# Attention stage of a three-block kernel: rounding, theta's high part and the sink columns move to GpSimd, the back-turned product stays in its own bank, and theta starts five steps later

## The chip, the cores and the metric

The kernel runs on one core of a Trainium2 chip. The metric is device time in microseconds (us) from the first to the last instruction of the program with what lies around it, and less is better. A kernel's time is the median of its runs.

## The reference, cut to what matters

```python
scores = q @ k.T / 8                    # 2 batches, 8 heads, 768 positions, 64 dims
scores = where(is_sink | in_window, scores, -1e9)        # 4 sink columns, window 128
a = softmax(scores);  x = a @ v         # x: 2 x 768 x 512
theta = x @ w_theta                     # 512 x 512
y = w_tok_r @ (x * cos(theta)) + w_tok_i @ (x * sin(theta))
u = x + y;  u = u + relu(u @ w_ch)
u = u + real(fft2(u));  out = u + relu(layernorm(u) @ w_ch1) @ w_ch2
```

Everything is fp32, and the inputs of each product except attention's are cut in a high and a low part (fp32r), so that a product is three matmuls: high by high, high by low, low by high.

## The kernel before, in words

The work has one order written out by hand, and a scheduler inside the language then settles the order on each engine from its own times. Attention (`attn_banded`) runs over 12 blocks of 128 positions (n, six for each batch; i is the block's number in its batch), four steps s to a block, and a loop over s issues, in each step, pieces of different blocks:

- `score_mms` at even steps: four heads' scores against the window (and sink) columns, in four PSUM banks (`ps_sc`). `scores` follows: VectorE adds the mask and finds the minimum (L515), ScalarE takes the exponential (L519). Once a block, for i of 2 or more, the sink columns of all heads are copied to `psk` (L524).
- `turn` one step later: TensorE transposes the probabilities of two heads into one of two banks (`ps_tp`, a ring), ScalarE or VectorE copies them out (L552). In a block's last turn the sink columns are transposed too, into the next bank of the same ring (L555), and copied to `pst` (L558).
- `av` six steps after the block's first step: the products with v into the bank `ps_acc` ("oa" in the rows). `av_turn` one step later transposes the product back, into a bank of `ps_tp`, and `normalize` (L608 to L610, VectorE) makes x from it.
- `theta_gen`, spread over four steps (and a rest that is issued when the next one starts): x is transposed into a bank of `ps_tp`, ScalarE makes the high part `hi` (L801) and the copy `xT` (L803), GpSimd (for the first nine tiles) the low part (L211), TensorE does twelve matmuls into the bank `th`, ScalarE copies them out scaled (L817), VectorE rounds to whole turns in two instructions (L818, L819) and GpSimd subtracts (L820).
- Until the first theta starts, each step has two dummy matmuls (L651) on zeros into the bank `th`; nothing reads them.
- Weights come as 64-bit words in `raw` tiles; `pump` converts one (`conv`: L279 on ScalarE, L287, L288, L291 on VectorE) and fetches the next on SyncE's queue (L255). The four tiles of w_theta are pumped at the steps of `THS` and cut in two one step later (ScalarE and GpSimd). From step `P0B` to `P0E`, every third step pumps a tile of w_tok. `conv` has a second form for `low_act`, used in later stages of the kernel before: ScalarE makes the low bits (L282), and VectorE needs two instructions (L283, L291) in place of three.

The step at which theta of tile u starts is `first(u) = 4u + AL + 2 + max(T1, T0 - u)`, with AL 3 and T1 4. With T0 of 7 that is 12, 15, 18, 21, then every fourth step. After attention come the token mixing (`y_gen`), the channel product, the transform and the MLP, all of them streams of matmuls.

Of the kernel before, what the change touches and what calls it, by code (L numbers as in the profile page):

```python
# [15 lines left out]
ALU = mybir.AluOpType  # L16
# [5 lines left out]
BLK = 128 + SINK  # L22
PW = 256 + SINK
BIG = 8.0e9
MAGIC = 12582912.0
# [4 lines left out]
GROUPS = [0, 3, 1, 2]  # L30
NSLOT = 67
NSLOT2 = 8
T0 = 7
DEPTH = 3
NRAW = 3
NJIT = 12
# [3 lines left out]
C1E = 12  # L40
TLC = 1
WN = 7
P0B = 15
P0N = 3
P0E = 40
F0 = 0
F1 = 2
ETH = 9
# [3 lines left out]
T1 = 4  # L52
TD = 1
AH = 5
THS = (5, 7, 9, 11)
P1E = 11
P2F = 1
TL = 1
# [132 lines left out]
class _Body:  # L191
# [315 lines left out]
    def scores(self, n, hp):  # L507
        nc = self.nc
        i, c = self.seq[n][1], n % 3
        nb, sm, p = self.tn[n]  # L510
        wd = PW if i else 128
        mask = self.masks[min(i, 2) if c else (0, 1, 3)[min(i, 2)]]
        for u, sc in enumerate(self.scs.pop((n, hp))):
            h = 2 * hp + u
            nc.vector.tensor_tensor_reduce(  # L515
                out=sc[:, 0:wd], in0=sc[:, 0:wd], in1=mask, op0=ALU.add, op1=ALU.min,
                scale=-0.125, scalar=3.0e38, accum_out=nb[:, h:h + 1],
            )
            self.last_exp = nc.scalar.activation(  # L519
                p[:, h, 0:wd], sc[:, 0:wd], AF.Exp, bias=nb[:, h:h + 1], scale=-1.0, accum_out=sm[:, h:h + 1]  # L520
            ).ins
        if hp == 3 and i >= 2:
            psk = self.psk.next()
            self.rnd("a", psk, p[:, :, 128:BLK])  # L524
            self.pt[n, 5] = psk
        if hp == 3:
            q = self.q.pop(n)
            if n:
                self.give(q)

    def turn(self, n, hp):
        nc = self.nc
        b, i = self.seq[n]
        c = n % 3
        p = self.tn[n][2]
        tp = self.ps_tp.next().rearrange("p (a m) -> p a m", a=4)
        pt = self.take(4, 128)
        parts = []
        for u in range(2):
            x, y = p[:, 2 * hp + u, 0:128], p[:, 2 * hp + u, BLK:PW]  # L540
            if i:
                prev, cur = (x, y) if c else (y, x)
                parts.append((u, prev, n - 1))
                parts.append((u, cur, n))
            else:
                parts.append((u, x, n))
        k = len(parts)
        for a, (u, pp, _) in enumerate(parts):
            self.tr(tp[:, a, :], pp, self.ident)
            yield  # L550
        tail = 4 * n + hp >= 4 * len(self.seq) - 5
        self.ev[n, hp] = self.rnd("v" if tail else EPT[hp], pt[:, 0:k], tp[:, 0:k])  # L552
        self.pt[n, hp] = pt, [(u, m) for u, _, m in parts]
        if hp == 3 and i >= 2:
            tp = self.ps_tp.next()  # L555
            self.tr(tp[:, 0:128], self.pt.pop((n, 5)).rearrange("p h c -> p (h c)"), self.ident)
            pst = self.pst.next()
            self.ev[n, 4] = self.rnd("v" if tail else "a", pst, tp[:, 0:128])  # L558
            self.pt[n, 4] = pst
# [35 lines left out]
        self.rnd("a", self.oT, acc)  # L595

    def av_turn(self, n):
        tp = self.ps_tp.next().rearrange("p (a m) -> p a m", a=4)
        for a in range(4):
            self.tr(tp[:, a], self.oT[:, a], self.ident)  # L600
        self.give(self.oT)
        self.normalize(*self.seq[n], tp.rearrange("p a m -> p (a m)"), self.tn.pop(n)[1])
# [16 lines left out]
    def attn_banded(self):  # L619
        last = len(self.seq) - 1  # L620
        nc = self.nc
# [4 lines left out]
        nstep = 4 * (last + 1)  # L626
        for s in range(nstep + T0 + AL + 4):
            n, hp = divmod(s, 4)
            if n < last and hp == 0:
                b, i = self.seq[n]  # L630
                if n:
                    self.load_k(n + 1)
                    self.load_q(n + 1)
                    self.load_v(n + 1)
                if i == NS - 2 and b + 1 < B:
                    self.load_sink(b + 1)
            if s == nstep - 4:
                self.sz = self.s.carve(6)
            if s == AH:
                self.ahead(2)  # L640
            if n <= last and not s % 2:
                self.score_mms(n, hp)
            g, k = divmod(s - AVS, 4)
            if 0 <= g <= last and k == 0:
                self.av(g)
            turn = self.turn(*divmod(s - TL, 4)) if TL <= s < nstep + TL else iter(())
            if 0 < s < first(0):

                ref = self.pe
                for _ in range(2):  # L650
                    i = nc.tensor.matmul(  # L651
                        self.zth[:, 0:256], lhsT=self.zz[:, 0:128], rhs=self.zz, start=s == 1, stop=False,
                        skip_group_check=True,
                    ).ins
                    self.after(i, ref)
            if TF:
                next(turn, None)
            for _ in turn:
                pass
            g, k = divmod(s - AVS, 4)  # L660
            if 0 <= g <= last and k == 1:
                self.av_turn(g)
            if 0 <= g + 1 <= last and k == 3:
                self.av_sink(g + 1)
            self.hold = None
            if n <= last and not s % 2:
                self.scores(n, hp)
                self.scores(n, hp + 1)
            if s in (nstep + 1, nstep + 3):
                u = (s - nstep) // 2  # L670
                with self.paced(ref=self.ev[last, 0]) if u else self.tc.issue_after(self.last_exp):
                    self.trig_act(0, u)
                with self.paced(ref=self.tl if u else self.ev[last, 1]):
                    self.trig_mul(0, u, "v")
            for u in range(last):
                k = s - first(u)
                if k == 0:
                    for _ in th.pop(u - 1, ()):
                        pass
                    th[u] = self.theta_gen(*self.seq[u])  # L680
                if 0 <= k < 4:
                    next(th[u], None)
            if n < last:
                if s in MST:
                    with self.paced(ref=self.last_exp):
                        self.build_mask(1 + MST.index(s))
                if s == SKS:
                    with self.paced(ref=self.last_exp):
                        self.sink_cols(0, 0, 1, 2)
                if hp == 0:  # L690
                    if n == 1:
                        with self.paced():
                            self.sink_v(0)
                    elif n and self.seq[n][1] == 0:
                        self.sink_cols(b, 0, 1)
                        self.sink_v(b)
            if s in THS:
                self.pump(0, lag=0, ref=self.last_exp)
            elif s - 1 in THS:
                with self.paced(ref=self.last_exp):  # L700
                    self.weight_split("th", THS.index(s - 1))
            elif P0B <= s < P0E and s % P0N == 0:
                self.pump(12, lag=0, ref=self.last_exp)
            if s - nstep in TAIL:
                u = TAIL.index(s - nstep)
                with self.paced(ref=self.ev[last, u]):
                    self.weight_split("tok", 1, (0, 2, 1)[u])
                if u < 2:
                    self.pump(8, ref=self.tl)
            if LA:  # L710
                self.mark(LA)
            if nstep - 4 <= s < nstep - 1:
                with self.paced(ref=self.last_exp):
                    self.weight_split("tok", 0, s - nstep + 4)
# [78 lines left out]
    def theta_gen(self, b, i):  # L793
        nc = self.nc
        x = self.x[b, i]
        tp = self.ps_tp.next().rearrange("p (a m) -> p a m", a=4)
        for a in range(4):
            self.tr(tp[:, a, :], x[:, a * 128:(a + 1) * 128], self.ident)
        hi = self.take(4, 128, dt=F32R)
        lo = self.take(4, 128, dt=F32R)  # L800
        self.rnd("a", hi, tp)  # L801
        xt = self.xT[b][:, :, i * 128:(i + 1) * 128]
        nc.scalar.activation(xt, tp, AF.Copy)  # L803
        self.low("v" if 6 * b + i >= ETH else "p", lo, xt, hi)
        self.tl = nc.cur_bb.bb.instructions[-1]
        yield
        th = self.ps_th.next()
# [7 lines left out]
        self.give(hi, lo)  # L815
        ph, km = self.take(512), self.take(512)
        nc.scalar.activation(ph, th, AF.Copy, scale=INV2PI)  # L817
        nc.vector.tensor_scalar(km, ph, MAGIC, None, op0=ALU.add)  # L818
        nc.vector.tensor_scalar(km, km, MAGIC, None, op0=ALU.subtract)  # L819
        nc.gpsimd.tensor_tensor(ph, km, ph, op=ALU.subtract)  # L820
        self.give(km)
        self.ph[b, i] = ph
# [569 lines left out]
```

## Time and profile before

| | |
|---|---|
| median of 3 runs | 616.45 us (614.87 to 616.68) |
| the profiled execution | 616.94 us, span 615.1 us |
| TensorE busy in the span | 590.4 us (96%) |
| VectorE / ScalarE / GpSimd busy | 345.0 / 349.9 / 298.1 us |
| mean granted TensorE clock | 0.989 |

The span is from the first to the last instruction; 1.8 us of the profiled execution's time lie around it. [...] Attention takes about the first 150 us of the span.

### The profile page before, as it was taken

What the parts mean: (1) busy time and instruction counts of PE and PEld (TensorE: products, weight loads), DVE (VectorE), ACT (ScalarE), POOL (GpSimd) and SP (SyncE); (2) the same over time, 40 slices, a digit from 0 to 9 for tenths busy, and PEclk for the clock granted to TensorE, in tenths of its full rate; (3) what the DMA queues carried; (4) which work ended last, traced back from release to release, by engine and by line L of the source; (5) the groups of instructions that cost most, each with busy time, mean ns of one, the idle gap of its engine ahead of it and who ended that gap; (6) DMA issues with size and microseconds to landing.
All of it is one profiled execution on the core that took longest, in us unless ns stands there. A gap on an engine that the chain in (4) does not pass through costs nothing.

```text
span 615.1 us, 9745 instructions
## 1 busy us (share of the span) xinstructions
PE 590.4 (96%) x3586; PEld 513.0 (83%) x3586; DVE 345.0 (56%) x713; ACT 349.9 (57%) x787; POOL 298.1 (48%) x252
## 2 busy tenths in 40 slices
PE   8979998998999999999999999999999999999995
PEld 6656776776888899977899999998998999998994
DVE  5875678855899669994556955556234311121112
ACT  4675667877585465566578865437447543443430
POOL 1121221243464743615565755758847556656651
PEclk9979999999899999999999999999999999999998
DMA  7832424210223613520046651100000000010001
GB/s 226 313 122 86 137 70 146 78 36 1 90 83 104 180 38 100 179 96 2 0 120 204 196 167 36 53 0 1 1 0 35 19 1 1 0 53 2 0 1 58
DMA packets 23338, 46.63 MB, mean 76 GB/s; under 512 B 2512, under 2 KB 9552, under 8 KB 23280
## 3 DMA queue, kind: packets, MB, share of 16 engines
q1 hardware_dynamic: 22032, 43.74, 22.5%
q0 software_dynamic: 1248, 2.17, 1.2%
q8 instruction: 30, 0.49, 0.3%
q14 instruction: 28, 0.23, 0.1%
HBM read 42.75 MB, written 3.15 MB: 75 GB/s over the span
## 4 chain that ended last, share of the span: by engine, by line
PE 61%; DVE 5%; ACT 1%; POOL 1%; issue 0%; POOLq 0%; ACTq 0%
PE pc L221 24%; PE acc L221 20%; PE s L221 8%; PE bank L221 7%; PE s L226 2%; ACT t L206 1%; DVE t L211 1%; POOL t L211 1%; DVE t L1165 0%; DVE t L838 0%; DVE t L1006 0%; DVE t L1018 0%; ACT t L1087 0%; DVE t L1014 0%; DVE t L1072 0%
## 5 line engine op out<-in xcount | busy, mean ns | idle before, releaser
L211 POOL TENSOR_TENSOR t<-t 128x512 fp32r<-128x512 f32 x151 | 202.2, 1360 | 174.5 <-ACT t L206 140.8
L221 PE MATMUL acc<-t 128*128 128x512 f32 x648 | 178.6, 394 | 0.0
L206 ACT ACTIVATE t<-t 128x512 fp32r<-128x512 f32 x172 | 102.0, 625 | 71.5 <-PE acc L221 26.8
L221 PEld LDWEIGHTS acc<-t 128*128 128x128 f32 x648 | 116.5, 188 | 17.9
L221 PE MATMUL pc<-t 128*128 128x384 f32 (+1 forms) x672 | 124.9, 314 | 1.8 <-DVE t L610 0.8
L221 PEld LDWEIGHTS pc<-t 128*128 128x128 f32 x672 | 113.8, 188 | 11.9 <-DVE t L610 1.0
L1152 DVE SCALAR_TENSOR_TENSOR t<-pc,t 128x384 fp32r<-128x384 f32 x64 | 35.6, 557 | 123.5 <-ACT t L1151 122.1
L211 POOL TENSOR_TENSOR t<-xT,t 128x512 fp32r<-128x512 f32 x39 | 52.7, 1369 | 48.7 <-ACT t L206 27.8
L221 PE MATMUL s<-t 128*128 128x256 f32 (+3 forms) x492 | 70.5, 286 | 1.7 <-DVE st L1072 0.8
L221 PE MATMUL pc<-uh,t 128*128 128x384 f32 x256 | 70.6, 337 | 0.0
L221 PEld LDWEIGHTS s<-t 128*128 128x128 f32 x492 | 65.8, 190 | 4.9 <-DVE st L1072 1.0
L221 PE MATMUL bank<-t 128*128 128x512 f32 x216 | 66.0, 402 | 1.4 <-DVE t L211 0.9
L1151 ACT ACTIVATE t<-pc 128x384 fp32r<-128x384 f32 x64 | 31.3, 489 | 61.8 <-PE pc L221 59.1
L221 PEld LDWEIGHTS pc<-uh,t 128*128 128x128 f32 x256 | 46.2, 188 | 0.8
L279 ACT ACTIVATE raw<-raw 128x512 f32<-128x512 f32 x58 | 38.8, 674 | 13.8 <-DMA raw<-in_w_ch_dram 8.6
L820 POOL TENSOR_TENSOR t<-t 128x512 f32<-128x512 f32 x12 | 16.1, 1339 | 62.2 <-DVE t L819 35.7
L221 PEld LDWEIGHTS bank<-t 128*128 128x128 f32 x216 | 39.0, 190 | 8.1 <-DVE t L211 1.5
L221 PE MATMUL pc<-ul,t 128*128 128x384 f32 x128 | 43.0, 336 | 0.6 <-DVE ul L211 0.6
L519 ACT ACTIVATE p<-sc,nb 128x272 f32<-128x272 f32 (+1 forms) x72 | 33.2, 469 | 14.3 <-DVE nb L515 13.5
L221 PE MATMUL th<-t 128*128 128x512 f32 x132 | 37.2, 414 | 1.4 <-ACT t L206 1.3
L515 DVE CUSTOM_DVE_ANT_0 sc<-sc,m 128x272 f32<-128x272 f32 (+1 forms) x72 | 28.7, 438 | 7.8 <-PE sc L221 7.7
L206 ACT ACTIVATE t<-xT 128x512 fp32r<-128x512 f32 x36 | 21.1, 626 | 19.1 <-PE acc L221 7.4
(142 smaller groups left out, 834.9 us busy)
## 6 DMA issues: line engine op xcount, KB each, us to landing
raw<-in_w_ch_dram SPq DMA_DIRECT2D x36, 512.0 KB, 3.7
kst<-in_k_dram SPq DMA_DIRECT2D x12, 256.0 KB, 3.9
t<-in_v_dram SPq DMA_DIRECT2D x12, 256.0 KB, 5.1
raw<-in_w_tok_rT_dram SPq DMA_DIRECT2D x6, 512.0 KB, 3.6
raw<-in_w_tok_iT_dram SPq DMA_DIRECT2D x6, 512.0 KB, 3.5
out_dram<-t SPq DMA_DIRECT2D x12, 256.0 KB, 2.3
t<-in_q_dram SPq DMA_DIRECT2D x11, 256.0 KB, 3.6
raw<-in_w_theta_dram SPq DMA_DIRECT2D x4, 512.0 KB, 6.7
```

Source lines behind the costliest of these rows:

```text
L206: return nc.scalar.activation(o, i, AF.Copy).ins
L211: e.tensor_tensor(o, x, hi.bitcast(F32), op=ALU.subtract)
L221: i = self.nc.tensor.matmul(o, lhsT=lhsT, rhs=rhs, start=start, stop=stop, skip_group_check=True).ins
L226: self.chained(self.nc.tensor.transpose(o, x, ident).ins)
L279: nc.scalar.activation(hf, hf, AF.Copy, scale=2.0 ** -112)
L515: nc.vector.tensor_tensor_reduce(out=sc[:, 0:wd], in0=sc[:, 0:wd], in1=mask, op0=ALU.add, op1=ALU.min, scale=-0.125, scalar=3.0e38, accum_ ...
L519: self.last_exp = nc.scalar.activation(p[:, h, 0:wd], sc[:, 0:wd], AF.Exp, bias=nb[:, h:h + 1], scale=-1.0, accum_out=sm[:, h:h + 1]).ins
L820: nc.gpsimd.tensor_tensor(ph, km, ph, op=ALU.subtract)
L1151: nc.scalar.activation(hh, hp, AF.Relu)
L1152: self.hl = nc.vector.scalar_tensor_tensor(hl, in0=hp, scalar=0.0, in1=hh.bitcast(F32), op0=ALU.max, op1=ALU.subtract).ins
```

## The change

`T0` goes from 7 to 12, so theta starts at steps 17, 20, 23, 26, 29, 32, 35, 38 and then, as before, 41, 45 and 49; the dummy matmuls go on to step 16. The four tiles of w_theta are pumped at 6, 9, 12, 15, in the `low_act` form, and the nine pumps of w_tok come three steps later. `psk` is copied by GpSimd. The transposed sink columns and the back-turned product go into `ps_acc`'s one bank instead of `ps_tp`'s two. For the first nine tiles `hi` is made by GpSimd from `xT` instead of by ScalarE from PSUM. The rounding is one GpSimd instruction in place of two of VectorE, for all twelve tiles.

```diff
-T0 = 7
+T0 = 12
-P0B = 15
+P0B = 18
-P0E = 40
+P0E = 43
-THS = (5, 7, 9, 11)
+THS = (6, 9, 12, 15)
@@ scores
-            self.rnd("a", psk, p[:, :, 128:BLK])
+            nc.gpsimd.tensor_copy(psk, p[:, :, 128:BLK])
@@ turn
-            tp = self.ps_tp.next()
+            tp = self.ps_acc.next()
@@ av_turn
-        tp = self.ps_tp.next().rearrange("p (a m) -> p a m", a=4)
+        tp = self.ps_acc.next().rearrange("p (a m) -> p a m", a=4)
@@ attn_banded
+            self.low_act = s < P0B
@@ theta_gen
-        self.rnd("a", hi, tp)
+        late = 6 * b + i >= ETH
+        if late:
+            self.rnd("a", hi, tp)
         nc.scalar.activation(xt, tp, AF.Copy)
-        self.low("v" if 6 * b + i >= ETH else "p", lo, xt, hi)
+        if not late:
+            nc.gpsimd.tensor_copy(hi, xt)
+        self.low("v" if late else "p", lo, xt, hi)
...
-        nc.vector.tensor_scalar(km, ph, MAGIC, None, op0=ALU.add)
-        nc.vector.tensor_scalar(km, km, MAGIC, None, op0=ALU.subtract)
+        nc.gpsimd.tensor_scalar(km, ph, MAGIC, MAGIC, op0=ALU.add, op1=ALU.subtract)
```

## Rows read from the trace of the kernel before

**Rows 1.** The page: TensorE's granted clock in 40 equal slices of the span, in tenths.

```profile
PEclk9979999999899999999999999999999999999998
```

**Rows 2.** Stretches of the span: length, each engine's busy time (instructions), clock, DMA share, GB/s.

```profile
24.00:44.00 20.00, 15.06 (x106) 11.01 (x104) 16.00 (x50) 13.30 (x44) 3.91 (x3) 0.85 0.49 162
36.00:48.00 12.00, 9.64 (x67) 7.22 (x67) 8.22 (x25) 6.89 (x23) 2.55 (x2) 0.72 0.21 67
52.00:148.00 96.00, 91.05 (x711) 69.45 (x710) 65.38 (x211) 70.34 (x207) 27.18 (x21) 1.00 0.27 83
148.00:164.00 16.00, 13.32 (x87) 10.42 (x86) 14.12 (x23) 7.38 (x13) 4.30 (x5) 0.89 0.05 12
152.00:160.00 8.00, 7.08 (x53) 5.79 (x53) 8.00 (x13) 3.32 (x7) 4.30 (x5) 0.79 0.00 1
165.00:270.00 105.00, 104.32 (x665) 94.15 (x664) 89.86 (x113) 62.62 (x108) 54.53 (x43) 1.00 0.39 118
0.00:150.00 150.00, 138.33 (x1009) 104.82 (x1009) 100.51 (x335) 100.89 (x305) 35.64 (x33) 0.98 0.39 125
```

**Rows 3.** What TensorE waited for from 20 to 52 us: total, times, longest.

```profile
PE sc L221 <- ACT p L519: 3.3, 2, 1.9
PE tp L226 <- DVE t L207: 1.5, 1, 1.5
```

**Rows 4.** Timeline of TensorE: start, duration, instruction, idle time before it and releaser.

```profile
39.32 1.81 PE L221 MATMUL sc<-kst,t 64*128 64x288 f32 x5 [1.88 <-ACT p L519]
```

**Rows 5.** VectorE's groups by shape, 16 to 45 us: conversions of five raw tiles.

```profile
L287 DVE TENSOR_SCALAR t<-raw 128x512 int32<-128x512 int32 x5 | 4.8, 951 | 3.3 <-ACT raw L279 3.2
...
L288 DVE SCALAR_TENSOR_TENSOR t<-raw,t 128x512 int32<-128x512 int32 x4 | 2.8, 689 | 0.1
L291 DVE SCALAR_TENSOR_TENSOR t<-raw,t 128x512 int32<-128x512 int32 x4 | 2.7, 685 | 0.0
```

**Rows 6.** ScalarE's instruction of the other form of conversion, whole span.

```profile
L282 ACT ACTIVATE raw<-raw,below 128x512 int32<-128x512 uint32 x33 | 25.0, 758 | 0.0
```

**Rows 7.** Timeline of TensorE's weight loads: one step's dummies, and what follows them.

```profile
20.15 0.73 PEld L651 LDWEIGHTS th<-z 128*128 128x128 f32 x4
20.91 0.57 PEld L226 LDWEIGHTS tp<-ident,p 128*128 128x128 f32 x4
```

**Rows 8.** VectorE's two rounding instructions, 0 to 172 us.

```profile
L819 DVE TENSOR_SCALAR t<-t 128x512 f32<-128x512 f32 x11 | 4.6, 422 | 0.0
L818 DVE TENSOR_SCALAR t<-t 128x512 f32<-128x512 f32 x11 | 4.6, 421 | 2.3 <-ACT t L817 2.3
```

**Rows 9.** ScalarE's groups by shape, 0 to 172 us: the high part of theta's x, and the sink columns.

```profile
L206 ACT ACTIVATE t<-tp 128x512 fp32r<-128x512 f32 x11 | 6.6, 602 | 1.3 <-PE tp L226 1.3
...
L206 ACT ACTIVATE psk<-p 128x128 f32<-128x128 f32 x8 | 2.6, 322 | 0.0
```

**Rows 10.** GpSimd's groups by shape, 0 to 150 us: theta's low part.

```profile
L211 POOL TENSOR_TENSOR t<-xT,t 128x512 fp32r<-128x512 f32 x9 | 12.1, 1340 | 20.9 <-ACT xT L803 16.7 <-DVE t L207 4.2
```

**Rows 11.** What TensorE waited for from 52 to 148 us: three of five.

```profile
PE oa L221 <- ACT pst L206: 1.9, 3, 0.9
PE th L221 <- ACT t L206: 1.3, 2, 0.9
...
PE tp L226 <- ACT t L206: 0.3, 1, 0.3
```

**Rows 12.** What SyncE's DMA queue waited for, 0 to 172 us: the longest.

```profile
SPq L255 <- DVE t L291: 98.9, 16, 37.8
```

**Rows 13.** Timeline of TensorE: theta's first products of the second tile.

```profile
55.31 0.73 PE L221 MATMUL th<-t 128*128 128x512 f32 x2 [0.92 <-ACT t L206]
```

**Rows 14.** Timeline of TensorE: the score matmuls of steps 18 and 42.

```profile
56.52 0.95 PE L221 MATMUL sc<-kst,t 64*128 64x272 f32 x5
...
124.53 0.95 PE L221 MATMUL sc<-kst,t 64*128 64x272 f32 x5
```

**Rows 15.** The first conversion instruction, 0 to 160 us: least, median and longest duration in ns.

```profile
L287 DVE TENSOR_SCALAR t<-raw x15: 415/427/1125, 17.0 to 159.0; 128x512 int32<-128x512 int32 x15
```

## The prediction

> **What bounds the kernel now.** I read first the granted clock over the span. It is full nearly everywhere; only the third slice (7) and the eleventh (8) of a stretch that is attention fall short, and the last [rows 1]. Then the busy times by stretch [rows 2]. From 165 to 270 us TensorE is busy for 104.32 of 105 us at full clock: the token mixing and what follows are a stream of matmuls, and a microsecond saved ahead of them comes off the end. So the question is how much TensorE loses in attention. It loses in three places:
>
> - A, 24 to 44 us: 20.00 - 15.06 = 4.9 us idle. After the gap the clock is low: from 36 to 48 us the mean is 0.72, which over 12 us is 3.4 us of full-speed work lost, and I count 2.8 of it, since part of the low stretch is the gap itself [rows 2]. The gap ends at 39.32 us with score matmuls that waited 1.88 us for the exponentials [rows 4], and the waits of this stretch are all on exponentials and on a VectorE copy [rows 3]. VectorE is the cause: it is busy for 16.00 of the 20 us [rows 2], and five conversions stand between its mask operations [rows 5].
> - B, 52 to 148 us: 96.00 - 91.05 = 4.9 us idle in small pieces, at full clock [rows 2], behind ScalarE and VectorE, never behind a transfer [rows 11].
> - C, 148 to 164 us: 16.00 - 13.32 = 2.7 us idle, and from 152 to 160 us a mean clock of 0.79, which is 8 x 0.21 = 1.7 us. VectorE is busy for 8.00 of those 8 us [rows 2].
>
> Together 7.7 + 4.9 + 4.4 = 17.0 us are lost. That is the ceiling of what any relief of the other engines can bring; the change also adds work to TensorE.
>
> **The change, part by part.**
>
> *More dummies.* Steps 12 to 16 get two dummies each, ten matmuls. One step's dummies begin at 20.15 us and the next weight load comes at 20.91 us, so a step pays 0.76 us [rows 7], and five pay 3.8 us. Where TensorE would stand idle they are free (lower bound 0); in those steps it has lost little but the gap, so I take all 3.8.
>
> *Conversions of w_theta later, and in the other form.* In the old form each has three VectorE instructions: between 16 and 45 us 0.95, 0.69 and 0.69 us, 2.3 in all [rows 5]; four are 9.3 us, crowded in seven steps. Two instructions of 0.69 us are 1.4 us, and by step 11 only two tiles have been done instead of four: VectorE has 9.3 - 2.8 = 6.5 us less in the stretch where it was busy for 80% [rows 2]. ScalarE pays 0.76 us more for each [rows 6], 3.0 us in all, against a busy time of 13.30 in 20 us; it is covered by ScalarE's idle third, and if that cover went it would delay exponentials by as much. The gap and the low clock behind it should mostly go: of A's 7.7 us I take three quarters, 5.8 us. Bounds: 7.7 if no gap is left, 2.8 if only the clock comes back.
>
> *Rounding.* VectorE loses 2 x 0.42 us for each of eleven tiles before 172 us, 9.3 us [rows 8]. GpSimd gains an instruction with one tensor input that the trace does not show at this size. Bounds: 0.42 us, VectorE's time for it [rows 8], and 1.34 us, GpSimd's with two inputs [rows 10]; I take 0.9, between them. GpSimd is the engine with room, 35.64 busy of 150 us [rows 2]. The result is the turned angle, which sine and cosine need much later, so a longer chain costs nothing there; only tile 11's lies in the next stage, where GpSimd is busy for about half of the time [rows 2].
>
> *High part.* ScalarE loses 0.60 us for each of nine tiles, 5.4 us [rows 9]; GpSimd gains nine copies at 0.42 to 1.34 us, again 0.9. The first product of theta now waits for `xT` and the copy instead of ScalarE's first instruction: +0.9 us for the high part and +0.3 for the low one. It is covered by the step (2.83 us: steps 18 to 42 take 124.53 - 56.52 = 68.0 us [rows 14]) that lies between transposes and products; without it, nine tiles cost up to 0.9 us each, 8 us.
>
> *Sink columns.* ScalarE loses 8 x 0.32 us, 2.6 us [rows 9]; GpSimd gains eight small copies, above 0 and below 1.34 us [rows 10], say 0.45. Two steps lie before they are transposed.
>
> GpSimd's additions come to 9 x 0.9 + 9 x 0.9 + 8 x 0.45 = 20 us in the first 150, so it would be at 37%; at the upper bounds 45%.
>
> *Own bank.* Sink transposes and the back-turned product leave the ring of two banks, which then serves only the turns and theta. In the one bank the order is product, its copy, back-turn, normalize, sink transposes, their copy, next product; each waits for its neighbour by its data, except the sink transposes, which wait for normalize. In the ring they were two banks behind the back-turned product's too, so no wait is new. I give it no term of its own: it is a reason to take part of B and C.
>
> *Later theta, later pumps.* The same twelve matmuls and four transposes for a tile, but a tile every third step from 17 to 41 instead of every fourth from 21. TensorE has more to do per step there and less idle time to fill. x of the first tiles is ready long before it is wanted, which helps. On SyncE's queue each fetch is issued behind the conversion that frees its buffer (98.9 us of waits [rows 12]), and loads of q, k and v stand behind it; all move by a few steps, and no wait of TensorE in B is on a transfer [rows 11], so 0. One pump of w_tok more comes near the end, where GpSimd's rounding has taken more off VectorE than it adds.
>
> *B and C.* VectorE and ScalarE are each relieved by about 8 us over 165 us, against 65.38 and 70.34 busy of 96 [rows 2]. I take 30% of B, 1.5 us (bounds 0 and 4.9), and a third of C, 1.5 us (0 and 4.4): in C VectorE is full and loses two or three tiles' rounding, 0.84 us each.
>
> Sum: 3.8 - 5.8 - 1.5 - 1.5 = -5.0 us. From the profiled execution's 616.94 this gives 611.9; the median of the runs shown is 616.45, 0.5 us lower, so **611.4 us**. Own range, with A at 2.8 to 7.7 and B and C at their bounds within reason: 606 to 614.
>
> [...] VectorE's first conversion instruction lasts 415 ns at the least and 1125 at the longest [rows 15], and 951 in the mean in the stretch where GpSimd cuts w_theta [rows 5]: 0.7 us is lost when something stands in its way. [...]
>
> **The rivals.**
>
> *Everything goes (-13).* All 17.0 us come back, for 3.8 us of dummies: 616.45 - 13.2 = 603.2. For it speaks that VectorE is named in all three places, against it that B's waits have several releasers [rows 11]. Below 606: chance 0.12.
>
> *Overlaps eat the gain.* When a tile follows after three steps, the rest of the one before is done in the step of its transposes. At the first such place in the kernel before, theta's products waited 0.92 us for the high part [rows 13]. The change has eight such places where there were three: 5 x 0.92 = 4.6 us, which leaves -0.4: 616.0. Against it: in all of B there are two such waits, 1.3 us together [rows 11]. Chance 0.13.
>
> [...] Chance 0.07.
>
> *GpSimd's chain becomes the wait (slower).* Rounding, subtraction, high part and low part of neighbouring tiles fall in one step on GpSimd: 2 x 1.34 + 2 x 0.9 = 4.5 us against a step of 2.83 [rows 10, 14]. If GpSimd takes them in the order of the program, the next tile's parts come 1.7 us after its products are wanted, and TensorE stops there; with eight such places 13 us, so 616.45 - 5.0 + 13 = 624. It decides as soon as the chain outlasts the step and the scheduler has put no other TensorE work between. For it: the subtraction comes ahead of the next tile's parts in the program. Against it: in the trace a tile's first two products, for which the high part is enough, were let go alone [rows 13], so the scheduler does place them by when their inputs come. Chance 0.14. [...]
>
> **How the numbers follow.** 0.3% of 616.45 is 1.85 us, about what a measurement of this kernel can tell from no change; so faster is below 614.6 and slower above 618.3. The forecast has 0.50. Faster: 0.50 + 0.12 + 0.06 (the better part of the two middle rivals) = 0.68. Same: the other 0.14. Slower: 0.14, and 0.04 for a new order elsewhere in the kernel, which the scheduler may give: 0.18. The range takes in half of the large gain, down to 604, and the nearer part of the slower cases, which spread from 618.3 upwards, up to 620: that leaves some 0.06 below and 0.13 above.
>
> **What would show it.** In the profile after: right, if TensorE's idle time between 24 and 44 us falls below 1.5 us and the clock stays full there; dummies of ten more matmuls, at 0.76 us a step; rounding and high part on GpSimd at 0.4 to 1.3 us; the token mixing begins about 5 us sooner, and nothing after it differs. Wrong, if TensorE waits for GpSimd's L820 or L211 in attention, if theta's products show gaps of 1 us or more every third step, if conversions on VectorE lengthen above 1 us in the mean, or if the gap of A returns at another step with its low clock. The prediction fails most easily in the clock: one new gap of 2 us can cost 3 us more behind it.

## The result and the profile after

The changed kernel takes 607.12 us (median of 4 runs, 606.89 to 608.64) against 616.56 us before, a ratio of 0.986 with a 95% interval of 0.983 to 0.988. The forecast was 611.4 us, -5.0 against the 616.45 us shown; it came to -9.4. One of the five executions of the run u1 below took 2604 us and is left out of its ratio.

The page of the changed kernel, the same line as [rows 1]: the clock is full in every slice of attention.

```profile
PEclk9999999999999999999999999999999999999998
```

The stretches of [rows 2], and the two that cover the same work as B and C there now that it comes sooner (columns as there):

```profile
24.00:44.00 20.00, 20.00 (x162) 15.42 (x161) 13.79 (x43) 14.35 (x41) 3.12 (x4) 1.00 0.59 179
36.00:48.00 12.00, 12.00 (x97) 9.33 (x97) 7.84 (x26) 8.24 (x25) 2.49 (x3) 1.00 0.50 153
165.00:270.00 105.00, 103.75 (x664) 93.25 (x663) 90.37 (x120) 61.07 (x107) 52.07 (x41) 1.00 0.37 112
0.00:150.00 150.00, 143.66 (x1077) 110.54 (x1079) 100.21 (x322) 100.71 (x299) 67.84 (x63) 1.00 0.40 125
...
45.00:138.00 93.00, 90.00 (x705) 69.34 (x706) 62.37 (x191) 61.72 (x188) 51.04 (x44) 1.00 0.29 86
138.00:153.77 15.77, 14.06 (x101) 10.84 (x98) 11.68 (x17) 10.45 (x21) 10.95 (x7) 1.00 0.01 1
```

A has no idle time left, B 93.00 - 90.00 = 3.0 us, C 15.77 - 14.06 = 1.7 us, all at full clock. The gap with the score matmuls behind it [rows 4] is gone. Four markers in the timelines of TensorE say where the time was won. First the kernel before, then the changed one: the warm-up matmuls, the first score matmul, the first product of token mixing into its banks `pc` (in both kernels six into `bank` come earlier), and the first long run of matmuls in the transform that follows.

```profile
1.26 6.27 PE L391 MATMUL bank<-z 128*128 128x256 f32 x14 [1.26 <-DVE z L389]
...
7.46 0.37 PE L221 MATMUL bank<-xT 64*128 64x128 f32 x1
...
163.63 0.62 PE L221 MATMUL pc<-t 128*128 128x256 f32 x3 [0.78 <-DVE t L610]
...
231.06 5.92 PE L221 MATMUL s<-t 128*128 128x256 f32 x48
```

```profile
1.27 4.94 PE L391 MATMUL bank<-z 128*128 128x256 f32 x14 [1.27 <-DVE z L389]
6.13 0.37 PE L221 MATMUL bank<-xT 64*128 64x128 f32 x1
...
153.77 0.60 PE L221 MATMUL pc<-t 128*128 128x256 f32 x3
...
221.09 5.92 PE L221 MATMUL s<-t 128*128 128x256 f32 x48
```

The last three moved by 1.33, 9.86 and 9.97 us, and the spans differ by 615.1 - 605.2 = 9.9: all of it was won before the products into `pc`. The first 1.33 us is no work of the change. It lies in the warm-up matmuls ahead of the first score (6.27 against 4.94 us), which the change does not touch; over the fourteen profiles of this study the first score matmul starts anywhere from 5.97 to 7.53 us. From here on I therefore compare **the span less the start of the first score matmul**: 607.6 us before, 599.1 after, -8.5. It is taken from one profiled execution of each kernel, and where that one lay far from the median it is said.

That is the whole balance, from the first score to the first product into `pc`. Before: 156.17 us, of which 12.9 idle and about 4.5 lost to the low clock (2.8 in A, 1.7 in C). After: 147.64 us, of which 5.1 idle, and no low clock. TensorE's busy time fell by 0.7 us, which is 3.8 us of dummies less the 4.5 of clock.

The clock's 4.5 us belongs to that execution of the kernel before. Its mean clock over the span was 0.989. Of 50 more executions of it, on four chips beside the runs below, the four at 0.989 took 616.6 us in the mean and the three at 0.999 took 614.4: those with next to no low clock are only about 2 us shorter. The changed kernel's 607.1 us is below all of them.

GpSimd's groups by shape, 0 to 150 us, of the changed kernel: the rounding, the subtraction, the high part and the sink columns.

```profile
L823 POOL TENSOR_SCALAR t<-t 128x512 f32<-128x512 f32 x10 | 20.1, 2013 | 12.5 <-ACT t L822 12.4
...
L824 POOL TENSOR_TENSOR t<-t 128x512 f32<-128x512 f32 x10 | 12.7, 1273 | 0.2
...
L808 POOL CAST t<-xT 128x512 fp32r<-128x512 f32 x9 | 6.5, 721 | 22.7 <-ACT xT L806 19.7 <-PE sc L221 1.8 <-PE tp L226 1.2
L524 POOL COPY psk<-p 128x128 f32<-128x128 f32 x8 | 2.3, 289 | 7.8 <-ACT p L519 7.8
```

The high part is 0.72 us, within the bounds; the rounding is 2.0 us, above the upper one (1.34). What TensorE still waits for, 24 to 150 us: one wait of 0.7 us is on GpSimd, the rest is small.

```profile
PE sc L221 <- ACT p L519: 1.0, 3, 0.4
...
PE th L221 <- POOL t L211: 0.7, 1, 0.7
```

### The profile page after: what moved, and what is told of

Its sections match the earlier page's. It is cut to its first block, busy times and chain, and to the rows that moved or that the text cites. A ratio compares the mean times of both kernels' runs of the same rounds, so it can differ in the third digit from the quotient of the medians.

```text
span 605.2 us, 9829 instructions
## 1 busy us (share of the span) xinstructions
PE 588.4 (97%) x3606; PEld 513.1 (85%) x3606; DVE 335.2 (55%) x685; ACT 345.4 (57%) x774; POOL 332.8 (55%) x281
## 4 chain that ended last, share of the span: by engine, by line
PE 83%; DVE 8%; ACT 5%; issue 1%; POOL 1%; DMA 0%; ACTq 0%; DVEq 0%; POOLq 0%
PE pc L221 26%; PE acc L221 22%; PE s L221 9%; PE bank L221 8%; PE oa L221 3%; PE th L221 3%; PE tp L226 3%; PE sc L221 2%; PE th L651 2%; PE s L226 2%; ACT p L519 1%; ACT t L206 1%; POOL t L211 1%; PE bank L391 1%; DVE t L211 1%
## 5 line engine op out<-in xcount | busy, mean ns | idle before, releaser
L221 PE MATMUL th<-t 128*128 128x512 f32 x132 | 35.9, 408 | 0.7 <-POOL t L211 0.7
L823 POOL TENSOR_SCALAR t<-t 128x512 f32<-128x512 f32 x12 | 25.4, 2117 | 16.2 <-ACT t L822 16.1
```

The source lines that it names most:

```text
L221: i = self.nc.tensor.matmul(o, lhsT=lhsT, rhs=rhs, start=start, stop=stop, skip_group_check=True).ins
L823: nc.gpsimd.tensor_scalar(km, ph, MAGIC, MAGIC, op0=ALU.add, op1=ALU.subtract)
```

## The experiments

All are edits of the kernel before ("before +") or of the changed one ("after"). Ratios are to the kernel before on the same chip, with 95% intervals. "Length" is the span less the first score's start, and its two parts are from there to the first product into `pc`, and from that to the long run of the transform; what follows is 383.8 to 384.5 us in every run. Idle is TensorE's, and the clock is the granted one. The profiled executions of s1 and s3 took 1.3 and 1.7 us more than their medians, so their lengths are long by about as much; the others lie within 0.8 us.

| run | edit | median us | ratio (interval) | length | its two parts | idle and clock, 24 to 45 us | idle, 45 to 138 us |
|---|---|---|---|---|---|---|---|
| before | - | 616.6 | 1 | 607.6 | 156.2, 67.4 | 4.9, 0.84 | 4.9 |
| after | - | 607.1 | 0.986 (0.983 to 0.988) | 599.1 | 147.6, 67.3 | 0.0, 1.00 | 3.0 |
| s1 | before + theta's start alone | 618.5 | 1.004 (1.003 to 1.006) | 611.2 | 158.9, 68.5 | 4.2, 0.92 | 7.0 |
| s2 | before + whole schedule | 613.8 | 0.996 (0.995 to 0.998) | 605.1 | 153.5, 67.4 | 0.3, 1.00 | 7.3 |
| s3 | before + GpSimd moves and bank | 611.6 | 0.993 (0.990 to 0.995) | 605.5 | 151.2, 70.2 | 4.9, 0.84 | 4.6 |
| v2 | before + bank alone | 615.5 | 0.999 (0.998 to 1.000) | 607.1 | 150.5, 72.5 | 4.5, 0.84 | 4.0 |
| u1 | after without the bank | 621.1 | 1.008 (1.006 to 1.011) | 613.8 | 160.5, 68.8 | 0.4, 1.00 | 8.1 |
| v1 | after, sink transposes in the ring | 612.1 | 0.992 (0.991 to 0.994) | 603.4 | 147.2, 72.2 | 0.0, 1.00 | 2.8 |
| u2 | after, rounding on VectorE | 612.6 | 0.994 (0.992 to 0.997) | 604.9 | 150.7, 70.0 | 0.0, 1.00 | 5.0 |
| u3 | after, high part on ScalarE | 610.6 | 0.991 (0.988 to 0.994) | 602.4 | 149.4, 68.6 | 0.0, 1.00 | 4.8 |
| u4 | after, old form of conversion | 607.9 | 0.987 (0.984 to 0.990) | 599.8 | 147.9, 67.4 | 0.0, 1.00 | 3.3 |
| s4 | after, dummies to step 11 | 605.1 | 0.982 (0.979 to 0.985) | 596.6 | 144.8, 67.3 | 1.6, 1.00 | 3.0 |
| v3 | after, one dummy a step, to 11 | 602.3 | 0.977 (0.975 to 0.978) | 594.5 | 143.0, 67.3 | 2.3, 0.95 | 2.0 |
| w1 | after, no dummies | 603.5 | 0.981 (0.978 to 0.983) | 595.7 | 144.0, 67.3 | 3.0, 1.00 | 3.0 |

All of them share one limit: each edit lets the scheduler settle the order on every engine anew, so a difference holds the edit and the new order together.

**s1, theta's start and the dummies alone.**

```diff
-T0 = 7
+T0 = 12
```

> Only theta's start at step 17 and the dummies up to step 16, on the kernel before (616.5 us). Theory V (the gap of A comes from VectorE, crowded by four conversions in seven steps): the crowding stays, so the gap and the low clock stay for the most part, and the dummies add up to 3.8 us: 615 to 620, idle in 24 to 45 us above 2 us. Rival D (the gap closes because dummies take the place of theta's early steps): idle below 1 us and full clock in 24 to 45 us, 609 to 613.

Slower, 618.5 us, and the gap is still there. The stretches 24 to 45 and 45 to 138 us of this run:

```profile
24.00:45.00 21.00, 16.83 (x121) 12.52 (x121) 17.46 (x53) 14.01 (x45) 3.81 (x3) 0.92 0.47 152
45.00:138.00 93.00, 86.00 (x682) 65.71 (x677) 60.11 (x196) 62.10 (x190) 22.84 (x18) 1.00 0.29 92
```

VectorE is busy for 17.46 of 21 us, and TensorE idle for 4.2 with dummies to hand: they don't close the gap. Rival D falls. Theta every third step also raises B's idle time from 4.9 to 7.0 us.

**s2, the whole schedule.**

```diff
-T0 = 7
+T0 = 12
-P0B = 15
+P0B = 18
-P0E = 40
+P0E = 43
-THS = (5, 7, 9, 11)
+THS = (6, 9, 12, 15)
+            self.low_act = s < P0B
```

> The whole schedule (theta at 17, dummies to 16, conversions of w_theta at 6, 9, 12, 15 in the form with two VectorE instructions, w_tok three steps later), nothing on GpSimd and no own bank. Theory V: A comes back whole (7.7 us) and the dummies cost 3.8, B and C stay: 616.5 - 3.9 = 612.6, with 611 to 614. Rival K (the ring of two banks makes the gap, through transposes that wait for a VectorE copy): the gap stays, 615 to 620.

613.8 us, as theory V has it: A's idle time falls to 0.3 us and the clock stays full, without the bank and without GpSimd. But B, which was to stay, is at 7.3 us, so part of A's gain is spent there.

```profile
24.00:45.00 21.00, 20.67 (x171) 15.88 (x169) 14.91 (x47) 15.76 (x47) 3.46 (x3) 1.00 0.55 175
45.00:138.00 93.00, 85.70 (x657) 65.29 (x658) 63.62 (x209) 65.47 (x201) 27.04 (x21) 1.00 0.29 89
...
111.25 0.66 PE L226 MATMUL tp<-ident,p 128*128 128x128 f32 x4 [1.43 <-DVE t L610]
```

The last row is a turn that waits for the normalize of a back-turned product: both banks of the ring are taken. At the end the first product into `pc` waits 1.82 us for the last normalize, where the kernel before waits 0.78.

**s3, the moves to GpSimd and the bank, old schedule.**

```diff
# of the changed kernel, these stay as before:
+T0 = 7
+P0B = 15
+P0E = 40
+THS = (5, 7, 9, 11)
-            self.low_act = s < P0B
```

> The moves to GpSimd and the own bank, with the schedule of the kernel before (theta at 12, conversions crowded in steps 5 to 11). Theory V: the gap of A stays, B and C give 2 to 4.7 us: 612 to 615, a low clock after the gap. Rival K: the gap is gone without the dummies being paid for: 605 to 609.

611.6 us, a little better than theory V's 612 to 615, and far from rival K's 605 to 609. The gap and its clock are the ones of before (first row; the second is this run's):

```profile
24.00:45.00 21.00, 16.07 (x111) 12.01 (x109) 16.04 (x51) 14.30 (x47) 4.46 (x4) 0.84 0.48 159
24.00:45.00 21.00, 16.12 (x107) 11.46 (x107) 16.52 (x49) 14.05 (x44) 6.38 (x7) 0.84 0.46 152
```

**s4, dummies only to step 11, theta still at 17.**

```diff
-            if 0 < s < first(0):
+            if 0 < s < 12:
```

> The changed kernel (607.1 us) with dummies only to step 11, theta still at 17. If the ten dummies are pure cost on a full TensorE: 607.1 - 3.8 = 603.3, 602.5 to 605. If they fill what would be idle and hold the clock: idle and a low clock appear between 30 and 48 us, and the time is 606 to 611.

605.1 us, at the upper edge of the first case: the length falls by 2.4 us and 1.6 us of idle time appear in A. Together 4.0 us, which is the dummies' work; so in the changed kernel they cost 2.4 and fill 1.6. The clock stays full without them.

**u1, the changed kernel without its own bank.**

```diff
 # turn
-            tp = self.ps_acc.next()
+            tp = self.ps_tp.next()
 # av_turn
-        tp = self.ps_acc.next().rearrange("p (a m) -> p a m", a=4)
+        tp = self.ps_tp.next().rearrange("p (a m) -> p a m", a=4)
```

> The changed kernel (607.1 us; 147.6 us from the first score matmul to the first product of token mixing) with the sink transposes and the back-turned product in the ring of two banks again. The schedule alone left 7.3 us idle between 45 us and the last stretch, the changed kernel 3.0. If the bank makes that difference: 609.5 to 613, with TensorE waits on normalize (L610) and on copies out of the ring. If GpSimd's relief makes it: 606.5 to 608.5.

621.1 us, slower than either case and than the kernel before. A is still closed; the loss is behind it: 8.1 us idle in B, 5.4 from 138 us to the first product into `pc`, and a low clock behind the longest gaps (0.60 from 96 to 100 us, 0.51 from 168 to 172). Three places from this run's timeline (TensorE, ScalarE, VectorE), and the stretch that follows the second:

```profile
84.65 0.60 PE L226 MATMUL tp<-ident,t 128*128 128x128 f32 x4
...
86.43 0.68 DVE L610 TENSOR_TENSOR t<-tp,rs 128x512 f32<-128x512 f32 x1
...
92.51 0.66 PE L226 MATMUL tp<-ident,t 128*128 128x128 f32 x4
...
95.62 0.60 ACT L806 ACTIVATE xT<-tp 128x512 f32<-128x512 f32 x1
...
96.27 0.65 PE L226 MATMUL tp<-ident,p 128*128 128x128 f32 x4 [2.15 <-ACT xT L806]
...
166.69 1.01 PE L221 MATMUL pc<-t 128*128 128x256 f32 x3 [3.49 <-DVE t L610]
```

```profile
96.00:100.00 4.00, 3.73 (x16) 2.31 (x16) 1.73 (x8) 2.90 (x10) 2.08 (x3) 0.60 0.36 124
```

A back-turned product sits in one of the two banks from 84.65 to 87.1 us, 2.5 us, until VectorE comes to it behind a conversion. Theta's x sits in a bank from 92.51 to 96.2, until ScalarE comes to `xT` at 95.62, behind exponentials; the next turn waits 2.15 us for it, and the clock falls to a mean of 0.60 behind the gap. The longest wait, 3.49 us, is at the end: the first product into `pc` waits for the last normalize. In every run with the back-turned product in the ring (before, s1, s2, u1) it waits so, for 0.8 to 3.5 us; in every run with the own bank it starts ahead of that normalize. From 45 to 170 us TensorE's waits for the ring's banks come to 6.0 us here, 2.9 of them on `xT`, 1.5 on `pst` and 1.6 on other copies, against 0.3 us in the changed kernel. None of these is on the back-turned product itself.

**v1, only the sink transposes back in the ring.**

```diff
 # turn
-            tp = self.ps_acc.next()
+            tp = self.ps_tp.next()
```

> The changed kernel with only the sink transposes back in the ring of two banks; the back-turned product stays in its own bank. If the ring is lost to the back-turned product (its bank is free only after normalize, on VectorE): 606.5 to 609, close to the changed kernel. If the sink transposes are what blocks the ring (their copy stands behind exponentials on ScalarE): most of the 13.5 us, 614 to 621.

612.1 us, between the two cases. In attention it is as good as the changed kernel (2.8 us idle in B, first product into `pc` 147.2 us after the first score, against 147.6): so with the back-turned product in its own bank the ring bears the sink transposes, as the first case has it. The other way round, only the sinks out of the ring, was not run. The 4.3 us of length are lost at one place in token mixing. VectorE's last instructions before the last normalize, and GpSimd's (POOL) that falls beside them, first of this run, then of the changed kernel, in the same order:

```profile
151.05 3.47 DVE L842 TENSOR_TENSOR t<-t 128x512 f32<-128x512 f32 x2
...
155.27 2.31 POOL L823 TENSOR_SCALAR t<-t 128x512 f32<-128x512 f32 x1 [1.30 <-ACT t L822]
...
155.72 1.69 DVE L288 SCALAR_TENSOR_TENSOR t<-raw,t 128x512 int32<-128x512 int32 x2
...
157.33 2.35 DVE L291 SCALAR_TENSOR_TENSOR t<-raw,t 128x512 int32<-128x512 int32 x2
...
159.60 0.68 DVE L610 TENSOR_TENSOR t<-oa,rs 128x512 f32<-128x512 f32 x1
...
160.34 0.65 PE L226 MATMUL s<-ident,t 128*128 128x128 f32 x4 [3.95 <-DVE t L610]
```

```profile
149.36 2.38 DVE L842 TENSOR_TENSOR t<-t 128x512 f32<-128x512 f32 x2
...
152.93 1.28 DVE L288 SCALAR_TENSOR_TENSOR t<-raw,t 128x512 int32<-128x512 int32 x2
...
154.14 1.28 DVE L291 SCALAR_TENSOR_TENSOR t<-raw,t 128x512 int32<-128x512 int32 x2
154.30 2.90 POOL L823 TENSOR_SCALAR t<-t 128x512 f32<-128x512 f32 x1 [3.71 <-ACT t L822]
155.34 0.68 DVE L610 TENSOR_TENSOR t<-oa,rs 128x512 f32<-128x512 f32 x1
...
156.07 0.66 PE L226 MATMUL s<-ident,t 128*128 128x128 f32 x4 [0.66 <-DVE t L610]
```

The same six instructions take 7.51 us there and 4.94 here. GpSimd is at work beside nearly all of them there (150.53 to 153.97 us, and from 155.27 on); in the changed kernel it is idle from 150.58 to 154.30. The transposes of the last tile wait 3.95 us instead of 0.66, 3.3 us more, and behind the wait the clock is 0.60 from 160.75 to 165 us, which costs some 1.7. Attention gives 0.4 of it back.

**v2, the own bank alone on the kernel before** (the edit of u1, turned round).

> The kernel before with only the own bank, for both uses. If the ring of two banks holds TensorE up whatever the schedule: faster by 3 to 5 us, 611 to 613, about as the moves and the bank together. If it counts only with theta every third step and the longer GpSimd chain: within 1.5 us of before, 614 to 617. The gap of A and its low clock stay in both.

615.5 us: hardly a change, the second case. But in the profiled execution that is a gain and a loss. The first product into `pc` comes 5.6 us sooner after the first score than before (150.5 against 156.2), and the stretch from there to the transform is 5.0 us longer (72.5 against 67.4). In that stretch TensorE waits twice for VectorE, for the last normalize and for a low part:

```profile
160.90 0.66 PE L226 MATMUL s<-ident,t 128*128 128x128 f32 x4 [1.69 <-DVE t L610]
...
189.49 0.50 PE L221 MATMUL bank<-t 128*128 128x512 f32 x1 [2.08 <-DVE t L211]
```

Behind the second wait the mean clock is 0.60 from 190 to 194 us. So the bank does help ahead of token mixing; the waits for VectorE in it take that back.

**u2, the rounding on VectorE again.**

```diff
-        nc.gpsimd.tensor_scalar(km, ph, MAGIC, MAGIC, op0=ALU.add, op1=ALU.subtract)
+        nc.vector.tensor_scalar(km, ph, MAGIC, None, op0=ALU.add)
+        nc.vector.tensor_scalar(km, km, MAGIC, None, op0=ALU.subtract)
```

> The changed kernel with the rounding as two VectorE instructions again. GpSimd's one instruction took 2.0 us, more than the upper bound of the prediction. If relief of VectorE counts: slower by 1 to 3 us, 608 to 610, idle in the last 16 us before token mixing above the 1.7 of the changed kernel. If the long GpSimd instruction costs as much as it frees (it delayed theta's low part once, 0.7 us): 605.5 to 607.5.

612.6 us, slower by more than the 1 to 3 us expected. VectorE's busy time from 45 to 138 us is 69.3 us against 62.4, and TensorE's idle time 5.0 against 3.0; there is a wait of 2.5 us for a copy by VectorE, which the changed kernel doesn't have. That is 2.0 of the 5.8 us of length; the clock is 0.91 in the mean from 138 us to the first product into `pc`, and 2.7 us more pass from there to the transform. The wait, among TensorE's from 45 to 150 us:

```profile
PE oa L221 <- DVE pst L207: 2.5, 1, 2.5
```

**u3, the high part on ScalarE for all tiles.**

```diff
-        if late:
-            self.rnd("a", hi, tp)
+        self.rnd("a", hi, tp)
...
-        if not late:
-            nc.gpsimd.tensor_copy(hi, xt)
```

> The changed kernel with theta's high part on ScalarE for all tiles. ScalarE has 5.4 us more over 90 us in which it was busy for 61 to 67%: if it is covered, 606.5 to 608; if the exponentials come later by it, 608 to 612. If GpSimd's chain was a cost, 605.5 to 606.5.

610.6 us, the second case: 1.8 us more idle in B, and a gap near 60 us (TensorE is busy for 1.76 of the 4 us from 60 to 64) after which the clock falls (0.57 from 64 to 68 us; mean 0.91 from 56 to 76 us).

**u4, the old form of conversion at the new steps.**

```diff
-            self.low_act = s < P0B
```

> The changed kernel with the old form of conversion for w_theta (three VectorE instructions), at the new steps. Theory V (VectorE's load makes the gap): some idle returns between 24 and 45 us, 1 to 3 us, and with a low clock if it comes in one piece: 608 to 612. If the spacing of the conversions alone is enough: idle there stays 0 and 606.5 to 608.

607.9 us, the second case: A stays closed with VectorE at 16.04 of 21 us instead of 14.79. That is as much as in the kernel before (16.04 too, in the first row at s3): the gap comes from where the conversions stand, not from how busy VectorE is. The spacing is enough here; without the new form the length is 0.7 us more, and the intervals of the ratios overlap.

**v3, one dummy a step, to step 11.**

```diff
-            if 0 < s < first(0):
+            if 0 < s < 12:
...
-                for _ in range(2):
+                for _ in range(1):
```

> The changed kernel with one dummy a step instead of two, up to step 11 instead of 16. Dummies stopped at step 11 gave 605.1. One dummy less in eleven steps is 11 x 0.4 = 4.4 us of TensorE work, of which a part becomes idle time: 602 to 605. If a gap then lets the clock fall: 605 to 610, with a mean clock below 0.95 between 10 and 48 us.

602.3 us, the first case and the fastest median of all: 0.977 (0.975 to 0.978) of the kernel before, and 4.6 us shorter than the changed one. Some clock is lost (0.95 from 24 to 45 us), less than the dummies cost.

**w1, no dummies.**

```diff
-            if 0 < s < first(0):
+            if False:
```

> The changed kernel without any dummies in attention's steps. Two a step up to 16 gave 607.1, two up to 11 gave 605.1, one up to 11 gave 602.3. If they are only work on TensorE: 602.3 less most of another 4.4 us, 598 to 601.5. If they hold the clock: the mean granted clock between 8 and 48 us falls below 0.9, each 4 us at 0.5 costs 2, and the time is 602.5 to 612.

603.5 us, above the first case and no better than v3. It lies in the second case's range, but the mean clock from 8 to 48 us is 0.96, not below 0.9: the clock falls once, early, and TensorE is idle for nearly half of a later stretch (TensorE alone: busy, clock, DMA share, GB/s).

```profile
12.00:16.00 4.00, 3.77 (x22) 0.63 1.05 398
20.00:24.00 4.00, 2.21 (x14) 1.00 1.03 354
```

## Why the prediction was right, and where its steps failed

The place and the sign are as forecast: all of the gain lies before the products into `pc`, and the matmuls behind fill TensorE before and after alike (104.32 and 103.75 busy of 105 us). Its size is not quite: -8.5 us of length against the sum's -5.0; the other 1.3 us of the profiled pair is the start. The sum held neither a loss that the new schedule brings nor what the own bank gives back (below); that it still came this near is in part luck.

**The terms**, as the profiled pair has them.

| term | forecast | measured | from |
|---|---|---|---|
| dummies | +3.8 | +2.4 net (4.0 of work, 1.6 of it in idle time) | s4 |
| A | -5.8 | -7.7, all of it | idle 4.9 to 0.0, and 2.8 of clock |
| B | -1.5 | -1.9 | idle 4.9 to 3.0 |
| C | -1.5 | -2.7 | idle 2.7 to 1.7, and 1.7 of clock |

C was sized too small: the prediction took a third of its 4.4 us, and all 1.7 of the clock came back with 1.0 of the idle time. A was taken at three quarters and came to the upper bound. With the forecast's 3.8 for the dummies' work the measured terms sum to 3.8 - 7.7 - 1.9 - 2.7 = -8.5, the length's change. With their net cost of 2.4 instead, A's term is 6.1 and not 7.7: the other 1.6 of its idle time is what they fill.

**A: the mechanism holds, one part of its working doesn't.** That VectorE's crowded conversions make the gap is shown: the new steps and form of w_theta's conversions, with w_tok's three steps later, closed it without the bank and GpSimd (s2, 4.9 to 0.3), and neither the dummies and theta's start (s1, 4.2 left), nor GpSimd and the bank (s3, 4.9), nor the bank alone (v2, 4.5) did. But the prediction counted the two-instruction form as part of the relief. In the changed kernel the gap stays shut without it (u4, 0.0); the fewer conversions by step 11 are enough there. And it argued from VectorE being busy for 80%: u4 has no gap with VectorE as busy as before.

**The step that failed: "Own bank. ... I give it no term of its own".** It counted that no wait is new, which holds, and did not ask how long each holder keeps a bank. Alone the bank is in sum worth nothing that can be told (v2, -0.5 us of length, interval 0.998 to 1.000). In the changed kernel its removal costs 14.7 us (u1, 613.8 against 599.1), more than the whole gain. The holders are named in u1's timeline: theta's x until ScalarE has come to `xT` (3.7 us at 92 us), and the back-turned product until VectorE's normalize (2.5 us at 85 us, 4.1 at 163 us, where token mixing waits for it). v1 divides it: with the back-turned product out of the ring, attention is whole, so that part is enough there. How much of the 14.7 us is the banks' and how much the new order is not shown. So the new schedule needs the bank: alone it wins A and loses 2.4 us in B (s2, 4.9 to 7.3), for a net 0.4%. That loss was not in the prediction, which gave "Later theta" 0 beyond the dummies. The moves to GpSimd and the bank without the new schedule leave A as it is and win 2.1 us of length in the profiled execution, about 4 by the medians (s3).

**The moves to GpSimd.** The high part (0.72 us) and the sink columns (0.29) are within their bounds. The rounding is not: 2.0 us against 0.42 to 1.34. TensorE waits for GpSimd only once in attention, for 0.7 us, and the move is worth its price: with the rounding on VectorE the length is 5.8 us more (u2), with the high part on ScalarE 3.3 (u3). Both are more than their share of "B and C" allowed. GpSimd is busy for 67.84 of the first 150 us, 45%; the prediction had 37%, and its upper bounds come to 47%, not to the 45% that it gave.

**The rivals.** *Everything goes* came closest of them (-13.2 against -8.5), but 3.0 us in B and 1.7 in C remain. *Overlaps*: five more places at 0.92 us were to cost 4.6; TensorE's waits for the high or low part come to one of 0.7 us. *GpSimd's chain*: with 2.0 us for the rounding it is longer than the 4.5 us assumed (2.0 + 1.3 + 0.7 + 1.3 = 5.3, against a step of 2.83), and still it does not decide: the same wait of 0.7 us is all of it, as TensorE has other matmuls to do meanwhile. *VectorE's conversions, longer beside GpSimd* (the chance of 0.07): they did get longer, and in attention nothing followed from it. The conversions from 48 to 150 us, first before, then after:

```profile
L291 DVE SCALAR_TENSOR_TENSOR t<-raw,t 128x512 int32<-128x512 int32 x8 | 6.4, 801 | 0.1
L288 DVE SCALAR_TENSOR_TENSOR t<-raw,t 128x512 int32<-128x512 int32 x8 | 5.5, 689 | 0.2
L287 DVE TENSOR_SCALAR t<-raw 128x512 int32<-128x512 int32 x8 | 3.6, 445 | 3.5 <-ACT raw L279 3.3
```

```profile
L288 DVE SCALAR_TENSOR_TENSOR t<-raw,t 128x512 int32<-128x512 int32 x9 | 8.0, 894 | 0.2
L291 DVE SCALAR_TENSOR_TENSOR t<-raw,t 128x512 int32<-128x512 int32 x9 | 6.8, 754 | 0.2
L287 DVE TENSOR_SCALAR t<-raw 128x512 int32<-128x512 int32 x9 | 6.0, 662 | 2.4 <-issue 1.5 <-ACT raw L279 0.7
```

A tile's three instructions take 2.31 us instead of 1.94 (two of them longer, L291 shorter); nine tiles make 3.4 us. TensorE's idle time fell in the same stretch, so attention absorbs it. It is not absorbed where TensorE waits for VectorE's last instruction: v1's six lengthened instructions (7.51 us against 4.94) stand ahead of the normalize that the last transposes wait for. In the kernel before, conversions are longer where a GpSimd instruction runs:

```profile
21.75 1.26 POOL L211 TENSOR_TENSOR t<-t 128x512 fp32r<-128x512 f32 x1 [18.70 <-ACT t L206]
22.20 1.10 DVE L287 TENSOR_SCALAR t<-raw 128x512 int32<-128x512 int32 x1
...
60.54 0.43 DVE L287 TENSOR_SCALAR t<-raw 128x512 int32<-128x512 int32 x1
```

Of its thirteen L287 from 14 to 120 us, the five that began while a GpSimd instruction ran took 0.59 to 1.12 us and ended 0.28 or 0.29 us after it; the eight beside which none ran took 0.42 or 0.43. That GpSimd's work alone lengthens the changed kernel's conversions and v1's six instructions is argued from the overlap in time, not shown.

**What stays open.** The differences from leaving out one part (14.7, 5.8, 4.3, 3.3) add up to far more than the 8.5 us won. The parts depend on one another, and each run also holds a new order by the scheduler; how much of each is which, these runs don't separate. The moves to GpSimd without the bank, on the old schedule, and each move alone on it, were not run.

**A better version.** v3 keeps all of the change but the dummies, one a step and none after step 11: 602.3 us. No dummies at all come within 0.4% of it (w1, 0.978 to 0.983 against 0.975 to 0.978), two a step to step 11 are behind v3 (s4, 605.1). All the dummies of the changed kernel are some 16 x 0.76 = 12 us of work by [rows 7], an estimate, and leaving them all out wins 3.4 us of length: most of them fill what would be idle or keep the clock, and of the ten that the change adds 2.4 of 4.0 us are cost.

## What to carry to other kernels

A part that is worth nothing alone can carry the whole: try it by taking it out of the changed kernel (14.7 us lost here) as well as by adding it to the old one (0.5 us won), and look in the second case whether a gain in one stage was lost in the next. Of a ring of banks ask how long each holder keeps one, until which engine working in order comes to it, and not only who waits for whom. Work that only fills TensorE should be trimmed again after each relief: here one dummy a step up to step 11 gave a ratio of 0.977 where all of them gave 0.986.

## What had not been expected of the hardware

In the changed kernel GpSimd's instruction with one tensor input and two operations took 2.0 us in the mean at 128x512 float32, longer than its instruction with two tensor inputs on the same tile (1.27 us) and nearly three times its copy (0.72 us). The number of inputs does not order these three prices.

One gap of 2.15 us (u1, 96 us) was followed by a mean clock of 0.60 over the next 4 us, one of 2.08 us (v2, 189 us) by 0.60 from 190 to 194 us. It does not always come so: v2's gap of 2.40 us that ends at 140.34 us left the clock at 1.00. v3's attention, with 2.3 us of idle time in smaller pieces from 24 to 45 us, kept a mean of 0.95 there (0.87 from 40 to 44 us, 0.70 from 44 to 48).

The first score matmul, behind the same warm-up matmuls, starts between 5.97 and 7.53 us over the profiles of this study: 1.5 us, as much as some of the terms. Spans should be compared from a marker behind it.
